# A window-attention and two-MoE kernel: rounds of 2, 7 and 7 feature blocks instead of 4, 6 and 6, and q tiles earlier in the queue

## Chip, core and metric

The kernel runs on one core of one Trainium2 chip. The metric is the device time of one execution in microseconds; a profiled execution gives a trace of every engine besides.

## What is computed

Inputs are float32. Attention has 2 batches, 8 heads, 768 positions and a head size of 64. Each position attends to the keys less than 16 positions away and to 24 block summaries (blocks of 32):

```python
k_sum = k.reshape(B, H, nb, 32, D).max(axis=3)
v_sum = v.reshape(B, H, nb, 32, D).mean(axis=3)
scores = [local q.k/8 where |i-j| < 16, q.k_sum/8 + log(32)]
a = softmax(scores)            # sum + 1e-9
x = a @ [v, v_sum]             # to 1536 tokens x 512
x = relu(x @ w_in)**2 @ w_out                    # 512 -> 2048 -> 512
xn = x / rms(x) * rms_g
out = (silu(xn @ w_gate) * (xn @ w_val)) @ w_out2  # 512 -> 1536 -> 512
```

## The kernel before

**Tokens.** The 1536 tokens are 12 groups of 128, six to a batch. Groups count from 0; group 6 is the first of batch 1. Four groups make a chunk (NCH = 3 chunks of 512 tokens).

**Attention of a group g** is a chain through four functions. scores(g) multiplies q by the group's keys, held transposed in kT (one buffer: batch 1 overwrites batch 0). softmax(g) adds the mask, takes the maximum, the exponentials and the division on VectorE and ScalarE; EXPACT chooses between eight exponentials with the sum accumulated and one long exponential. ptrans(g) transposes the probabilities on TensorE. av(g) multiplies them by vx, the group's values with the block means appended, and split_xs writes the result as a high and a low part, xhi and xlo, which is what the products consume. qload(g) and qprep(g) fetch and transpose the q of two groups; vload(g) fetches a group's rows of v into vx by six transfers; prep_load, prep_k and prep_kend make kT; vmean, its copy vm on ScalarE and vmfix (transfers from vm into vx) make the block means.

**Weights.** A unit is one feature block of 128 features of one weight matrix. It arrives as raw words of the input (512 KB) and is converted by the Units class in a pipeline: load, conv_a on ScalarE, conv_b on VectorE (four steps), split into hi and lo on both. tick() moves each unit one step; until(u) ticks until u is ready. The list `order` sets the order, round by round. load(k) issues transfers up to the k-th unit; `cap` and `used` limit how far loading runs ahead. Weights, raw words, and the q, k and v tiles share 14 buffers of one tag; nine more come free when attention's memory is released.

**Feed-forward.** All products are three matmuls (hi by hi, hi by lo, lo by hi) per 128 rows. The 16 feature blocks of the first feed-forward are split into rounds (ROUNDS1); each round goes over all tokens and adds to yp. Round 0 runs beside attention in the loop over k_ (six steps, two groups each): h_pair(k_, f) computes two blocks for two groups (256 columns each) and squares, y_pair(k_, f) multiplies by w_out. TICKS gives the conversions at the end of each k_. The later rounds (steps1) run over chunks of 512 tokens after it, and then the second feed-forward (steps2).

**Order.** Instructions are queued on each engine in the order of the program as a list scheduler arranges it at build time: where an instruction's inputs would be late, a later one can be put ahead of it. On the chip each queue runs in order. All transfers are issued by SP's queue.

Of the kernel before, what the change touches and what calls it, by code (L numbers as in the profile page):

```python
# [14 lines left out]
AF = mybir.ActivationFunctionType  # L15
# [17 lines left out]
def tile_window_attention_moe_moe2(  # L33
# [13 lines left out]
    nc = tc.nc  # L47
# [19 lines left out]
    NG = NT // P  # L67
# [3 lines left out]
    NCH = NG // MT  # L71


    ROUNDS1 = [4, 6, 6]
    ROUNDS2 = [4, 4, 4]
    FIRST1 = [sum(ROUNDS1[:r]) for r in range(len(ROUNDS1))]
    FIRST2 = [sum(ROUNDS2[:r]) for r in range(len(ROUNDS2))]
# [121 lines left out]
    class Units:  # L199


        def __init__(self, units):
# [3 lines left out]
            self.ahead = 3  # L206
            self.used, self.cap = 0, 2 * ROUNDS1[0]

# [29 lines left out]
    def PARTS(g):  # L238
        return 2 if g < 3 else 1

    QB = 2
    TICKS = (0, 0, 1, 1, 2, 3)
    WARM = 10
    WOLAG = 2
    order = [("wi", f) for f in range(ROUNDS1[0])] + [("wo", f) for f in range(ROUNDS1[0])]
    for kinds, out_, rounds, firsts in (
        (("wi",), "wo", ROUNDS1, FIRST1), (("wg", "wv"), "wp", ROUNDS2, FIRST2)
    ):
# [25 lines left out]
    mark = {}  # L274

    def after(*marks):
        es = ExitStack()
        for m in marks:
            es.enter_context(tc.issue_after(mark[m].ins))
        return es  # L280
# [73 lines left out]
    def qload(g):  # L354
        b, r = divmod(g, GPB)
        state[("q", g)] = token_chunk(q, b, r // 2, f"qr{g}")
# [11 lines left out]
    def vmean(b, c):  # L368

        if c == 0:  # L370
            state["vmps"] = psA(f"vmean{b}", [NB, DM])
        ps = state["vmps"]
        pb = BLK // 2
        nb2 = P // pb
        vr = state.pop(("v", b, c))
        for e in range(2):
            nc.tensor.matmul(
                ps, ind[:, nb2 * (NC2 - 1 - c) : nb2 * (NC2 - 1 - c) + NB], vr[:, :, e, :],
                start=(c == 0 and e == 0), stop=(c == NC2 - 1 and e == 1),
            )  # L380
        if c == NC2 - 1:
            vm = ap_.tile([NB, DM], F32, tag="vm", name=f"vm{b}", bufs=1)
            nc.scalar.copy(vm, ps)
            state["vm"] = vm
            state[("vsum", b)] = True

# [10 lines left out]
    def vload(g):  # L397
        b, r = divmod(g, GPB)
        i0 = 2 * g % NVX
        for u in range(2):  # L400
            t0 = r * P + u * QT
            for j, n, o in ((0, WIN, t0 - WIN), (K0, QT, t0), (K1, WIN, t0 + QT)):
                o = min(max(o, 0), S - n)
                nc.sync.dma_start(  # L404
                    vx[j : j + n, i0 + u], v[b, :, o : o + n, :].rearrange("h s d -> s h d")
                )
# [19 lines left out]
    def softmax(g):  # L426
        r = g % GPB
        mk = masks["first" if r == 0 else ("last" if r == GPB - 1 else "mid")]
        sl = state.pop(("s", g))
        te = ap_.tile([P, 2, NPAIR, NK], F32, tag="t", name=f"t{g}", bufs=TB)  # L430
        t = te.rearrange("q e p n -> q (e p) n")
        state[("t", g)] = t
        mx = ap_.tile([P, H], F32, tag="mx", name=f"mx{g}", bufs=TB)
        sm = ap_.tile([P, H], F32, tag="sm", name=f"sm{g}", bufs=TB)
        parts = PARTS(g)
        n = H // parts
        for i in range(parts):
            hs = slice(n * i, n * i + n)
            tv, m_, s_ = t[:, hs], mx[:, hs], sm[:, hs]
            for e in range(2 // parts * i, 2 // parts * (i + 1)):  # L440
                nc.vector.tensor_tensor(
                    te[:, e], sl[e], mk.unsqueeze(1).to_broadcast([P, NPAIR, NK]), op=ALU.add
                )
            if EXPACT(g):
                nc.vector.reduce_max(m_, tv, axis=AX.X, negate=True)
                for h in range(hs.start, hs.stop):
                    mark[("exp", g)] = nc.scalar.activation(  # L447
                        t[:, h], t[:, h], AF.Exp, bias=mx[:, h : h + 1], accum_out=sm[:, h : h + 1]
                    )
            else:  # L450
                nc.vector.reduce_max(m_, tv, axis=AX.X)
                nc.vector.tensor_tensor(tv, tv, m_.unsqueeze(2).to_broadcast([P, n, NK]), op=ALU.subtract)
                mark[("exp", g)] = nc.scalar.activation(tv, tv, AF.Exp)
                nc.vector.reduce_sum(s_, tv, axis=AX.X)
            nc.vector.tensor_scalar_add(s_, s_, 1e-9)
            nc.vector.reciprocal(s_, s_)
            mark[("norm", g)] = nc.vector.tensor_tensor(
                tv, tv, s_.unsqueeze(2).to_broadcast([P, n, NK]), op=ALU.mult
            )
# [121 lines left out]
    def group(g):  # L581

        scores(g)
        if g > 3:
            vload(g)
        softmax(g)
        if g + 2 < NG and g % 2 == 0:
            qload(g + 2)


# [12 lines left out]
    for c in range(NC2):  # L603
        vm_load(0, c)
    vload(0)
    vload(1)
    qload(2)
    for j in (0, LK - WIN):
        nc.gpsimd.memset(kT[:, :, j : j + WIN], 0.0)
    prep_k(0, 0)  # L610
# [10 lines left out]
        vmean(0, c)  # L621
    vmfix(0, NVX // 2)
    with after("vmfix"):
        units1.load(8)
    softmax(1)
    rot["tags"] = ("a", "x")
# [39 lines left out]
    def h_pair(k_, f):  # L666
        ps = psB.tile([P, CH], F32, tag="h", name=f"h0_{k_}_{f}", bufs=2)
        m = 2 * k_ % MT
        for j in range(2):
            units1.until(("wi", f + j))  # L670
            product(ps[:, G2 * j : G2 * (j + 1)], W[("wi", f + j)], xs[(1, 2 * k_ // MT)], m, m + 2)
        t = square(ps, f"0_{k_}_{f}")
        hq[(k_, f)] = hsplit(t, CH, f"0_{k_}_{f}")

    def y_pair(k_, f, between=()):
        if f == 0:
            for m in range(2):
                ys[m] = y_tile(k_, m, "y0_")
        hh = hq.pop((k_, f))
        for j in range(2):  # L680
            units1.until(("wo", f + j))
            ff_out(
                [ys[m] for m in range(2)], [t[:, G2 * j : G2 * (j + 1)] for t in hh],
                W[("wo", f + j)], f + j == 0, f + j == ROUNDS1[0] - 1,
            )
            if between:
                between[j]()
        if k_ == NK2 - 1:
            units1.used += 4
        if f == ROUNDS1[0] - 2:  # L690
            for m in range(2):
                gather(2 * k_ + m, ys.pop(m), 0, ROUNDS1, "y", None)
# [3 lines left out]
    for k_ in range(NK2):  # L696
        g, last = 2 * k_ + 3, 2 * k_ + 3 >= NG
        if k_ == 0:
            for c in range(NC2):
                prep_load(1, c)  # L700
        h_pair(k_, 0)
        if k_ == 0:
            av(2)
            group(4)
        if not last:
            ptrans(g)
        if g == GPB - 1:
            group(GPB)
        h_pair(k_, 2)
        if not last:  # L710
            av(g)
        if g == GPB - 1:
            for c in range(NC2):
                vmean(1, c)
            vmfix(0, 1)
        if g + 2 < NG:
            group(g + 2)
            if g + 2 == GPB + 1:
                vmfix(1, 1)
        y_pair(k_, 0)  # L720
        if g + 1 < NG:
            ptrans(g + 1)
        if k_ == 0:
            prep_begin(1)
            prep_k(1, 0)
            y_pair(k_, 2, (lambda: prep_k(1, 1), lambda: prep_k(1, 2)))
            prep_kend(1, 0)
            prep_kend(1, 1)
            for c in range(NC2):
                vm_load(1, c)  # L730
        else:
            if g + 3 < NG:
                qprep(g + 3)
            y_pair(k_, 2)
        if g + 1 < NG:
            av(g + 1)
        if k_ == 0:
            qprep(GPB)
        elif g + 3 < NG:
            group(g + 3)  # L740
        if k_ == 2:
            units1.cap = NW - 3
        for _ in range(TICKS[k_]):
            units1.tick()
        if not last and g == NG - 1:
            actx.close()
            rot["tags"] = ("a",)
            side["pool"] = ctx.enter_context(
                tc.tile_pool(name="w2pool", bufs=1, side="right", reuse_waits="tile")
            )  # L750
            side["psum"] = ctx.enter_context(
                tc.tile_pool(name="psY2", bufs=1, space=PSUM, reuse_waits="tile")
            )
            grow = side["pool"].tile([P, DM], F32, tag="grow", name="grow")
            nc.sync.dma_start(grow, rms_g.partition_broadcast(P))
            units1.cap = NW + NRIGHT - 3
# [4 lines left out]
    for i in range(n1 + 2):  # L761
        if i < n1:
# [3 lines left out]
            ps = psB.tile([P, CH], F32, tag="h", name=f"h{c}_{f}", bufs=2)  # L766
# [92 lines left out]
```

## Time and profile before

| | us |
|---|---|
| time, median of 3 runs | 678.31 (677.69 to 678.68) |
| the profiled execution | 682.7 |
| its span, first to last instruction | 681.0 |
| TensorE busy | 654.7 (96%) |
| VectorE busy | 404.4 (59%) |
| ScalarE busy | 305.8 (45%) |

The profiled execution is 4.4 us over the median of the timed runs, and 1.7 us of it lie outside the span. Times in the trace count from the start of the span. Busy time of TensorE is modelled, and it includes time at the lower clock, in which the same matmul takes twice as long.

### The profile page before, as it was taken

The numbers are of one execution on the slowest core, as the hardware profiler recorded it, in microseconds if no ns is written. First come the engines' busy times: TensorE is split into PE (matmuls) and PEld (weight loads), VectorE is DVE, ScalarE is ACT, GpSimd is POOL, SyncE is SP. The second block draws the span as 40 slices with busy tenths as digits, with TensorE's granted clock in tenths as the row PEclk, the third lists the DMA queues.
The fourth block names the chain that finished last, engine by engine and source line by source line (L and its number), as shares of the span: only waits on it lengthen the run. The fifth ranks groups of instructions, "written<-read, shape, count | busy, mean of one in ns | idle before, by whom it ended". The sixth has DMA issues, their size and how long they took to land.

```text
span 681.0 us, 9361 instructions
## 1 busy us (share of the span) xinstructions
PE 654.7 (96%) x3644; PEld 533.9 (78%) x3644; DVE 404.4 (59%) x733; ACT 305.8 (45%) x637; POOL 4.1 (1%) x25
## 2 busy tenths in 40 slices
PE   7768998999999999999999999999999999999997
PEld 5456957888888888888888888888888888888885
DVE  4799758656999579726574795189613171313132
ACT  4597558365866447326352773167411131111110
POOL 2000000000000000000000000000000000000000
PEclk9769998999999999999999999999999999999999
DMA  9678556222522223001021251015300000001011
GB/s 244 147 247 190 131 171 160 68 49 91 189 62 94 93 63 123 31 1 62 13 98 46 68 180 62 1 34 162 113 1 1 0 1 0 1 1 62 1 62 63
DMA packets 78188, 54.22 MB, mean 80 GB/s; under 512 B 46080, under 2 KB 72704, under 8 KB 78144
## 3 DMA queue, kind: packets, MB, share of 16 engines
q1 hardware_dynamic: 78144, 53.62, 26.7%
q8 instruction: 29, 0.48, 0.3%
q14 instruction: 15, 0.12, 0.1%
HBM read 50.07 MB, written 3.15 MB: 78 GB/s over the span
## 4 chain that ended last, share of the span: by engine, by line
PE 86%; SPq 5%; DVE 4%; DMA 2%; ACT 1%; issue 1%; DVEq 0%; ACTq 0%
PE y L530 19%; PE h L509 18%; PE g L509 15%; PE v L509 15%; PE z L530 14%; SPq L404 3%; PE xps L488 1%; PE pps L467 1%; PE s L418 1%; SPq L303 1%; DMA raw_wo<-in_moe_w_out_dram 1%; PE xps L500 1%; ACT t L447 1%; SPq L292 1%; DMA raw_wi<-in_moe_w_in_dram 1%
## 5 line engine op out<-in xcount | busy, mean ns | idle before, releaser
L509 PE MATMUL h<-xhi,w_wi 128*128 128x512 f32 (+1 forms) x480 | 136.6, 357 | 1.8 <-ACT xhi L478 1.2
L530 PE MATMUL y<-w_wo,hhi 128*128 128x512 f32 x384 | 120.7, 398 | 1.9 <-ACT hhi L520 1.7
L805 DVE TENSOR_TENSOR sg<-v,sg 128x512 f32<-128x512 f32 x36 | 24.9, 692 | 134.8 <-PE v L509 134.8
L509 PEld LDWEIGHTS h<-xhi,w_wi 128*128 128x128 f32 x480 | 87.3, 195 | 15.7 <-ACT xhi L478 1.9
L509 PE MATMUL v<-xhi,w_wv 128*128 128x512 f32 x288 | 95.6, 393 | 0.0
L509 PE MATMUL g<-xhi,w_wg 128*128 128x512 f32 x288 | 95.4, 393 | 0.0
L530 PE MATMUL z<-w_wp,hhiz 128*128 128x512 f32 x288 | 89.0, 392 | 0.0
L509 PE MATMUL h<-xlo,w_wi 128*128 128x512 f32 (+1 forms) x240 | 86.1, 359 | 1.8 <-DVE xlo L479 1.8
L530 PEld LDWEIGHTS y<-w_wo,hhi 128*128 128x128 f32 x384 | 72.4, 190 | 18.2 <-ACT hhi L520 1.9
L530 PE MATMUL y<-w_wo,hlo 128*128 128x512 f32 x192 | 75.1, 401 | 0.0
L803 ACT ACTIVATE sg<-g 128x512 f32<-128x512 f32 x36 | 21.6, 600 | 104.6 <-PE g L509 102.4
L509 PEld LDWEIGHTS v<-xhi,w_wv 128*128 128x128 f32 x288 | 54.0, 188 | 12.3
L509 PEld LDWEIGHTS g<-xhi,w_wg 128*128 128x128 f32 x288 | 54.0, 188 | 12.3
L530 PEld LDWEIGHTS z<-w_wp,hhiz 128*128 128x128 f32 x288 | 54.0, 188 | 11.9
L657 ACT ACTIVATE r<-h 128x512 f32<-128x512 f32 x48 | 28.7, 598 | 71.3 <-PE h L509 71.2
L509 PE MATMUL g<-xlo,w_wg 128*128 128x512 f32 x144 | 56.6, 393 | 0.0
L509 PE MATMUL v<-xlo,w_wv 128*128 128x512 f32 x144 | 56.5, 393 | 0.0
L530 PE MATMUL z<-w_wp,hloz 128*128 128x512 f32 x144 | 55.9, 392 | 0.0
L509 PEld LDWEIGHTS h<-xlo,w_wi 128*128 128x128 f32 x240 | 46.9, 195 | 9.0 <-DVE xlo L479 2.4
L658 DVE TENSOR_TENSOR r<-h,r 128x512 f32<-128x512 f32 x48 | 33.0, 687 | 35.0 <-ACT r L657 35.0
L520 ACT CAST hhiz<-sg 128x512 fp32r<-128x512 f32 x36 | 22.4, 621 | 69.7 <-DVE sg L805 69.4
L530 PEld LDWEIGHTS y<-w_wo,hlo 128*128 128x128 f32 x192 | 36.2, 191 | 8.1 <-issue 0.2
(125 smaller groups left out, 897.5 us busy)
## 6 DMA issues: line engine op xcount, KB each, us to landing
raw_wi<-in_moe_w_in_dram SPq DMA_DIRECT2D x16, 512.0 KB
raw_wo<-in_moe_w_out_dram SPq DMA_DIRECT2D x16, 512.0 KB
raw_wg<-in_moe_w_gate_dram SPq DMA_DIRECT2D x12, 512.0 KB
raw_wv<-in_moe_w_val_dram SPq DMA_DIRECT2D x12, 512.0 KB
raw_wp<-in_moe_w_out_dram SPq DMA_DIRECT2D x12, 512.0 KB
kr<-in_k_dram SPq DMA_DIRECT2D x12, 256.0 KB
qr<-in_q_dram SPq DMA_DIRECT2D x12, 256.0 KB
vr<-in_v_dram SPq DMA_DIRECT2D x6, 512.0 KB
```

The costliest lines, as they stand in the source:

```text
L292: nc.sync.dma_start(t.rearrange("p h e d -> p h (e d)"), src[b, :, 2 * P * c : 2 * P * (c + 1), :].rearrange("h (p e) d -> p h (e d)", e=2),)
L303: nc.sync.dma_start(t[:, j].rearrange("p (h d) -> p h d", h=H), src[b, :, o : o + P, :].rearrange("h p d -> p h d"),)
L404: nc.sync.dma_start(vx[j : j + n, i0 + u], v[b, :, o : o + n, :].rearrange("h s d -> s h d"))
L418: mark[("s", g)] = nc.tensor.matmul(sl[e][QT * u : QT * u + QT, p, :], qT[rr, p, QT * u : QT * u + QT], kT[rr, p, o : o + NK], start=True, ...
L447: mark[("exp", g)] = nc.scalar.activation(t[:, h], t[:, h], AF.Exp, bias=mx[:, h : h + 1], accum_out=sm[:, h : h + 1])
L509: nc.tensor.matmul(ps, a_, b_, start=(i == 0), stop=(i == tot - 1))
L520: nc.scalar.copy(hi[:, 0:n], s[:, 0:n])
L530: nc.tensor.matmul(y, a_[:, ms], b_, start=(first and i == 0), stop=(last and i == 2))
L657: nc.scalar.activation(t, ps, AF.Relu)
L658: nc.vector.tensor_tensor(t, ps, t, op=ALU.mult)
L803: nc.scalar.activation(t, psg, AF.Silu)
L805: nc.vector.tensor_tensor(t, psv, t, op=ALU.mult)
```

## The change

ROUNDS1 becomes [2, 7, 7]: in the loop over k_, one h_pair and one y_pair run per step instead of two each, and the two blocks join the later rounds. Since `cap` and the beginning of `order` follow ROUNDS1[0], round 0 wants four units instead of eight, and units1.load(8) then fetches wi0, wi1, wo0, wo1, wi2, wi3, wi4, wo2. The one h_pair stands behind av(2), group(4), ptrans and, at GPB - 1, group(GPB). TICKS gets one more conversion, at k_ = 1. qload(2) is issued ahead of vload(1) instead of behind it, qload(4) right behind vmfix and ahead of the raw weights instead of within group(2). Group 1's exponentials are queued on ScalarE behind the copy vm.

```diff
--- before.py
+++ after.py
@@ -71,7 +71,7 @@
     NCH = NG // MT
 
 
-    ROUNDS1 = [4, 6, 6]
+    ROUNDS1 = [2, 7, 7]
     ROUNDS2 = [4, 4, 4]
     FIRST1 = [sum(ROUNDS1[:r]) for r in range(len(ROUNDS1))]
     FIRST2 = [sum(ROUNDS2[:r]) for r in range(len(ROUNDS2))]
@@ -239,7 +239,7 @@
         return 2 if g < 3 else 1
 
     QB = 2
-    TICKS = (0, 0, 1, 1, 2, 3)
+    TICKS = (0, 1, 1, 1, 2, 3)
     WARM = 10
     WOLAG = 2
     order = [("wi", f) for f in range(ROUNDS1[0])] + [("wo", f) for f in range(ROUNDS1[0])]
@@ -380,7 +380,7 @@
             )
         if c == NC2 - 1:
             vm = ap_.tile([NB, DM], F32, tag="vm", name=f"vm{b}", bufs=1)
-            nc.scalar.copy(vm, ps)
+            mark["vm"] = nc.scalar.copy(vm, ps)
             state["vm"] = vm
             state[("vsum", b)] = True
 
@@ -450,7 +450,8 @@
             else:
                 nc.vector.reduce_max(m_, tv, axis=AX.X)
                 nc.vector.tensor_tensor(tv, tv, m_.unsqueeze(2).to_broadcast([P, n, NK]), op=ALU.subtract)
-                mark[("exp", g)] = nc.scalar.activation(tv, tv, AF.Exp)
+                with after(*(["vm"] if g == 1 else [])):
+                    mark[("exp", g)] = nc.scalar.activation(tv, tv, AF.Exp)
                 nc.vector.reduce_sum(s_, tv, axis=AX.X)
             nc.vector.tensor_scalar_add(s_, s_, 1e-9)
             nc.vector.reciprocal(s_, s_)
@@ -584,7 +585,7 @@
         if g > 3:
             vload(g)
         softmax(g)
-        if g + 2 < NG and g % 2 == 0:
+        if g + 2 < NG and g % 2 == 0 and g > 2:
             qload(g + 2)
 
 
@@ -603,8 +604,8 @@
     for c in range(NC2):
         vm_load(0, c)
     vload(0)
+    qload(2)
     vload(1)
-    qload(2)
     for j in (0, LK - WIN):
         nc.gpsimd.memset(kT[:, :, j : j + WIN], 0.0)
     prep_k(0, 0)
@@ -621,6 +622,7 @@
         vmean(0, c)
     vmfix(0, NVX // 2)
     with after("vmfix"):
+        qload(4)
         units1.load(8)
     softmax(1)
     rot["tags"] = ("a", "x")
@@ -698,15 +700,13 @@
         if k_ == 0:
             for c in range(NC2):
                 prep_load(1, c)
-        h_pair(k_, 0)
-        if k_ == 0:
             av(2)
             group(4)
         if not last:
             ptrans(g)
         if g == GPB - 1:
             group(GPB)
-        h_pair(k_, 2)
+        h_pair(k_, 0)
         if not last:
             av(g)
         if g == GPB - 1:
@@ -717,13 +717,12 @@
             group(g + 2)
             if g + 2 == GPB + 1:
                 vmfix(1, 1)
-        y_pair(k_, 0)
         if g + 1 < NG:
             ptrans(g + 1)
         if k_ == 0:
             prep_begin(1)
             prep_k(1, 0)
-            y_pair(k_, 2, (lambda: prep_k(1, 1), lambda: prep_k(1, 2)))
+            y_pair(k_, 0, (lambda: prep_k(1, 1), lambda: prep_k(1, 2)))
             prep_kend(1, 0)
             prep_kend(1, 1)
             for c in range(NC2):
@@ -731,7 +730,7 @@
         else:
             if g + 3 < NG:
                 qprep(g + 3)
-            y_pair(k_, 2)
+            y_pair(k_, 0)
         if g + 1 < NG:
             av(g + 1)
         if k_ == 0:

```

## Rows read from the trace of the kernel before

**Rows 1.** The page, part 2: TensorE's busy tenths in 40 equal slices of the span.
```profile
PE   7768998999999999999999999999999999999997
```

**Rows 2.** Table of stretches (window, its length, busy us of each engine, clock, DMA).
```profile
0.00:28.10 28.10, 19.01 (x140) 13.29 (x141) 16.91 (x38) 13.28 (x33) 4.05 (x25) 0.91 0.81 198
28.10:87.70 59.60, 51.15 (x514) 43.74 (x513) 49.27 (x90) 41.37 (x107) 0.00 (x0) 0.87 0.70 186
87.70:162.20 74.50, 70.17 (x715) 56.74 (x714) 47.27 (x79) 44.90 (x134) 0.00 (x0) 0.95 0.37 98
162.20:681.00 518.80, 514.39 (x2278) 420.17 (x2278) 290.98 (x528) 206.24 (x365) 0.00 (x0) 1.00 0.18 58
```

**Rows 3.** Chain that ended last, in order of time: start us, us, what.
```profile
22.35 3.07 DMA qr<-in_q_dram
...
40.64 1.66 SPq L404
```

**Rows 4.** Timeline of SP's queue, 0 to 70 us: start us, us, line, transfer, count.
```profile
13.75 8.56 SPq L404 DMA_DIRECT2D vx<-in_v_dram  x12
22.35 1.06 SPq L303 DMA_DIRECT2D qr<-in_q_dram  x2
...
33.36 5.27 SPq L303 DMA_DIRECT2D qr<-in_q_dram  x2
38.72 10.29 SPq L404 DMA_DIRECT2D vx<-in_v_dram  x12
```

**Rows 5.** Chain that ended last, whole span: TensorE's pieces with their counts.
```profile
85.02 2.75 PE y L530 x12
...
147.41 4.51 PE h L509 x36
...
190.20 2.80 PE h L509 x12
```

**Rows 6.** Table of stretches for tile y alone.
```profile
40.00:87.70 47.70, 13.48 (x48) 8.64 (x48) 1.26 (x2) 0.59 (x1) 0.86 0.66 159
87.70:162.20 74.50, 20.03 (x73) 13.83 (x72) 2.18 (x4) 1.75 (x3) 0.95 0.37 98
```

**Rows 7.** Groups by line up to 162.2 us, VectorE: busy, mean ns, idle before.
```profile
L658 DVE TENSOR_TENSOR r<-h,r 128x512 f32<-128x512 f32 x10 | 6.9, 686 | 4.7 <-ACT r L657 4.7
...
L186 DVE SCALAR_TENSOR_TENSOR x_wi<-raw_wi,x_wi 128x512 uint32<-128x512 uint32 x7 | 4.7, 686 | 0.0
...
L182 DVE TENSOR_SCALAR x_wi<-x_wi 128x512 f32<-128x512 f32 x7 | 2.9, 420 | 4.9 <-ACT x_wi L175 4.8
```

**Rows 8.** Timeline of all engines, 24 to 31 us.
```profile
24.31 1.17 ACT L453 ACTIVATE t<-t 128x480 f32<-128x480 f32 x2 [2.58 <-DVE t L452]
...
25.39 0.56 ACT L383 COPY vm<-vmean 24x512 f32<-24x512 f32 x1
...
30.58 0.66 DVE L441 TENSOR_TENSOR t<-s,mask_mid 128x480 f32<-128x480 f32 x1 [2.49 <-PE s L418]
```

**Rows 9.** Timeline of TensorE and VectorE, groups 6, 10 and 11.
```profile
104.56 1.27 PE L488 MATMUL xps<-pT,vx 120*64 120x64 f32 x30
...
134.28 1.21 DVE L441 TENSOR_TENSOR t<-s,mask_mid 128x480 f32<-128x480 f32 x2
...
140.65 1.16 DVE L457 TENSOR_TENSOR t<-t,sm 128x960 f32<-128x960 f32 x1
...
142.93 1.21 DVE L441 TENSOR_TENSOR t<-s,mask_last 128x480 f32<-128x480 f32 x2
```

**Rows 10.** Table of stretches around the start of the next round.
```profile
250.00:280.00 30.00, 30.00 (x131) 24.41 (x130) 28.72 (x55) 20.44 (x35) 0.00 (x0) 1.00 0.29 88
```

**Rows 11.** Table of stretches of 10 us with a low granted clock (column after POOL).
```profile
20.00:30.00 10.00, 5.09 (x30) 4.14 (x30) 7.77 (x20) 5.75 (x17) 0.00 (x0) 0.66 0.51 106
40.00:50.00 10.00, 6.74 (x31) 5.94 (x30) 9.57 (x20) 8.70 (x27) 0.00 (x0) 0.51 0.66 163
110.00:120.00 10.00, 7.76 (x76) 6.01 (x75) 7.20 (x12) 7.39 (x24) 0.00 (x0) 0.76 0.84 214
```

## Prediction

> **What bounds the kernel now.** I read the page first: the 40 slices [rows 1]. TensorE's busy tenths fall short of 9 in five of the first seven slices and in the last, nowhere else. So the span falls into a part where attention sets the pace and a part that is pure TensorE work. The table of stretches [rows 2] makes that exact. I cut it at three places: 28.1 us (VectorE ends the softmax of group 1), 87.7 us (first scores of group 6, the first of batch 1) and 162.2 us (the last time TensorE waits for anything). The reader should see that TensorE is idle 9.1 us in the first stretch (28.1 - 19.01), 8.5 us in the second, 4.3 us in the third, and then only 4.4 us in 518.8, at the very end. Call the stretches S (start), A, B and C.
>
> The chain of waits [rows 3] says why A is slow. The q tile of groups 2 and 3 lands late; later TensorE does nothing useful until the window tiles vx of groups 2 and 3 have been issued on SP's queue. SP's own order [rows 4] shows why: qr(2) goes out at 22.35, behind twelve vx transfers; the raw weights follow, and the second qr pair (5.27 us for what took 1.06 us before) and vx stand behind seven 512 KB weight transfers. VectorE is meanwhile busy 49.27 of A's 59.6 us [rows 2], much of it converting weights, since eight are wanted before the first k_ step is through.
>
> **The change, part by part.** *Feed-forward moved.* A pair of blocks for two groups is 24 matmuls of 256 columns in h_pair and 12 of 512 in y_pair. The chain has 36 of the first kind in 4.51 us, so 24 in 3.0, and 12 of the second in 2.75 [rows 5]: 5.75 us a pair. There are 12 pairs now (six k_ times two) and six after, so 6 x 5.75 = 34.5 us of TensorE leave round 0. Two blocks join the later rounds: 2 x 3 chunks x 2 products of 12 wide matmuls at 2.75 to 2.80 us, taken as 2.77, which is 33.3 us. The form alone gains 1.2 us. Where they stand now: 48 y matmuls before 87.7 (4 pairs) and 73 from there to 162.2 (6 pairs, one matmul of them into the next) [rows 6]; two pairs lie in C. Half of each goes: 11.5 from A, 17.25 from B, 5.75 from C.
>
> *Weights.* Four conversions (wi2, wi3, wo2, wo3) are no longer wanted at once. One costs VectorE 0.42 + 0.42 + 0.69 + 0.69 + 0.69 = 2.9 us [rows 7], four 11.6; a pair costs it 0.69 + 0.69 = 1.37 [rows 7], and two pairs leave A, 2.7. VectorE in A falls from 49.3 to 34.9 us. Its idle time in A is 10.3 us, of which 2.49 is the wait for group 2's scores [rows 8].
>
> *q tiles and vm.* qload(2) passes vload(1)'s six transfers, so it goes out at about 18 instead of 22.35 (half of the 8.56 us of vx x12 earlier [rows 4]). Those six vx pass 1.06 us later, and are wanted only when group 1's attention product starts, past 34 us: no cost. VectorE is busy up to 28.1 anyway, so only the 2.49 us wait goes, not the full four. The new wait puts vm's copy ahead of group 1's exponentials on ScalarE. Behind it stand those exponentials and all of ScalarE's queue; but ScalarE sits idle 2.58 us before them, and the copy takes 0.56 [rows 8], so it fits in the gap: no cost, and if vmean came later than that gap the price would be up to 0.6. It frees vmfix (four transfers, 3.5 us on SP, from 25.98 now): SP is through with vload(1) at about 23.4, so they start there, 2.5 us earlier, and end near 27. qload(4) passes the seven raw weights, which brings it from 33.36 to there. The raw weights lose about 1 us of SP time to it and gain the 2.5. The last qload leaves the place ahead of vx(2), so vx(2) should start 3 to 5 us earlier; this is inside the A estimate, not added.
>
> *h_pair(0) behind av(2) and group(4), and one more tick at k_ = 1.* Both move work within A; the tick is one conversion of 2.9 us of VectorE. Priced at nothing for TensorE, because a conversion of a later round only fills VectorE's gaps; if that cover is gone it is 2.9 us of A.
>
> *A, summed.* VectorE 34.9 + idle left 7.8 (10.3 - 2.5) = 42.8 us instead of 59.6: A ends at 70.9, 16.8 earlier. From below, TensorE: 51.15 - 11.5 = 39.7. From above: three conversions of later blocks (the x32 buffers are three) are pulled forward without their last step, 3 x 2.2 = 6.6, so 49.4. I take 42.8, by VectorE's own row. Net of the 11.5 us that only moved, A gives 5.3 us.
>
> *B, summed.* It now lasts 74.5. With the moved pairs out and the same waits it would be 57.25. From below, TensorE's floor: 57.25 - 4.3 = 52.9. From above, the softmax chains as they run now, with nothing gained: the first group has its scores at 87.7 and its attention product is over at 105.8 (104.56 + 1.27) [rows 9], because v's means come between; two 512-wide steps like those of [rows 7] follow, so 19.4 us. The other five follow at the distance of two successive groups late in B, whose masks start at 134.28 and 142.93, 8.65 apart [rows 9]; within that the softmax itself, masks to the end of the division at 141.81, takes 7.5. 19.4 + 5 x 8.65 = 62.6. I take 59.0, nearer the upper end, because the means' transfers and product come earlier with A but get no shorter. That loses 1.75 us against 57.25.
>
> *C.* 518.8 - 5.75 + 33.3 = 546.3. A round now needs 14 weights instead of 12, two more conversions, 5.8 us, where VectorE was busy 28.72 of 30 us around a round's start [rows 10]: at worst 5.8 - 1.3 = 4.5 us. TensorE is busy all 30 us there and in C as a whole to its end [rows 2], so the weights come ahead of need, and I take zero.
>
> **Sum.** 28.1 + 42.8 + 59.0 + 546.3 = 676.2 us of span against 681.0: -4.8. The profiled run took 682.7, 4.4 above the median of the runs, so 677.9 on its scale and 678.3 - 4.8 = 673.5 on the median's.
>
> **The rivals.** (1) *Batch 1's attention loses its cover and sets the pace in B; slower.* For: now TensorE is idle only 4.3 us there, so the feed-forward does hide the softmax chain, and half of that goes. Against: VectorE is busy 47.27 and ScalarE 44.9 of 74.5 us [rows 2], so engines have room. Decides when B exceeds 57.25 + 5.3 + 1.2 = 63.75 us: with 19.4 for the first group, a period of 8.9. At a period of 10, B is 69.4 and the time 673.5 + 10.4 = 683.9.
>
> (2) *The clock falls with the cover; slower.* In three stretches of 10 us the granted clock was 0.66, 0.51 and 0.76 [rows 11], and the first of them holds the wait for qr [rows 3]. The loss is half of the busy time spent at 1.2 GHz: shares 0.68, 0.98 and 0.48 of 5.09, 6.74 and 7.76 us, or 1.7 + 3.3 + 1.9 = 6.9 us. If as much again is lost where attention now runs thinner, the time is 673.5 + 6.9 = 680.4. For: two of the three lie where little feed-forward is ready yet. Against: B as a whole is granted 0.95 [rows 2]. The Trainium skill (TensorE: Matmul & The Clock Gate, Loop structure matters more than you think) has the same rule: matmuls in dense succession keep the full clock, a wait between bursts loses it; by that rule a thinner attention stage ends slower, and the trace's 40 to 50 us agree with it, at 0.51.
>
> (3) *The front doesn't move; no change.* The transfers of vx(2) stay behind the raw weights, which still number seven, and VectorE fills itself with conversions (A 49.4, 6.6 more, or no gain from the queue at all). A then gives about nothing and the time is 673.5 + 5.3 = 678.8. For: SP issues in order. Against: group 4's scores need only its q tile, which moves ahead.
>
> (4) *B runs at TensorE's floor.* B 52.9, the time 673.5 - 6.1 = 667.4. For: engines' room as in (1), and round 1's first h products can fill gaps once their weights exist.
>
> **Chances.** The forecast (A shorter, B about as well covered) 0.42, its own range 670 to 676.5; rival 4 0.18; rival 3 0.15; rival 1 0.17; rival 2 0.08. A difference under 0.2% (1.4 us) can hardly be told from none here. So faster 0.60, same 0.15, slower 0.25. The range is 666 to 681.5: it takes in rivals 2, 3 and 4 and the lower part of 1, and leaves out a B paced at 10 us and a C that stalls.
>
> **What would show it.** Right: qr(2) issued near 18 us and vm's copy ahead of group 1's exponentials; VectorE's 2.49 us wait gone; first scores of group 6 near 71 us; the last TensorE wait near 130, and a C of about 546 without idle time; 144 matmuls of 256 columns on h. Wrong: group 6 past 76, or B over 63.75 with TensorE waiting for pT or xhi, or granted clocks near 0.5 between 71 and 130, or waits of TensorE for weights after the last group.

## The result, and the profile after

The change made the kernel slower: 690.0 us, median of 4 runs (689.45 to 691.21), against 678.5 for the kernel before; the ratio is 1.0137 with a 95% interval of 1.0103 to 1.0171. The profiled execution after is its median, with a span of 688.3 us; that of before, at 682.7, lay 4.2 us above the median of 678.5, so the two traces differ by 7.3 us where the medians differ by 11.5.

TensorE's busy time is the same in both traces, 655.1 us against 654.7. What grew is its idle time, from 26.3 (681.0 - 654.7) to 33.2 us. The 40 slices of the page after [rows 1]:

```profile
PE   7776969989999999999999999999999999999997
```

The table of stretches after (window, its length, busy us of PE, PEld, DVE, ACT, POOL, then clock, DMA share, GB/s), cut where its own stages end: first scores of group 6 at 75.4, end of TensorE's last wait and the matmul behind it at 147.6:

```profile
0.00:28.10 28.10, 20.88 (x168) 14.03 (x170) 17.57 (x39) 14.15 (x35) 4.03 (x25) 0.97 0.84 204
28.10:75.40 47.30, 36.09 (x404) 30.83 (x400) 41.53 (x79) 34.96 (x96) 0.00 (x0) 0.84 0.91 235
75.40:147.60 72.20, 62.15 (x656) 49.08 (x656) 56.65 (x97) 50.18 (x145) 0.00 (x0) 0.95 0.42 113
147.60:688.30 540.70, 536.01 (x2351) 436.56 (x2349) 289.60 (x520) 208.69 (x365) 0.00 (x0) 1.00 0.16 54
```

Read length minus PE in each row and set it beside [rows 2]: idle 7.2 (was 9.1) in S, 11.2 (8.5) in A, 10.1 (4.3) from there to the last wait, 4.7 (4.4) behind it. Of the 10.1 us, 8.0 lie before group 11's xlo is done at 137.7, which is where B ends as the prediction cuts it, and 2.0 are one wait behind it. A is 12.3 us shorter, but more work than that left it: 48 of its 96 h matmuls and 36 of its 48 y matmuls, 14.25 us at the prediction's prices. The idle time grew in A and nearly doubled in B.

The edits to the start did what they say. SP's queue after [rows 4]:

```profile
18.07 1.33 SPq L303 DMA_DIRECT2D qr<-in_q_dram  x2
...
23.38 3.46 SPq L393 DMA_DIRECT2D vx<-vm  x4
26.89 1.13 SPq L303 DMA_DIRECT2D qr<-in_q_dram  x2
...
34.66 4.92 SPq L404 DMA_DIRECT2D vx<-in_v_dram  x6
```

qr(2) goes out at 18.07, vmfix at 23.38, qr(4) at 26.89, and vx of group 2 at 34.66 instead of 38.72. On ScalarE and VectorE [rows 8], the timeline of 17 to 31 us:

```profile
20.98 0.58 ACT L383 COPY vm<-vmean 24x512 f32<-24x512 f32 x1
...
23.55 1.17 ACT L454 ACTIVATE t<-t 128x480 f32<-128x480 f32 x2 [1.99 <-DVE t L452]
...
27.24 0.65 DVE L441 TENSOR_TENSOR t<-s,mask_mid 128x480 f32<-128x480 f32 x1
...
29.38 0.66 DVE L441 TENSOR_TENSOR t<-s,mask_mid 128x480 f32<-128x480 f32 x1 [1.49 <-PE s L418]
```

The copy vm stands ahead of group 1's exponentials, and group 2's mask starts at 27.24 instead of 30.58; VectorE's 2.49 us wait is 1.49 us, for the second half of the scores.

Where the new idle time is, TensorE's timeline shows (in brackets the idle time ahead of the instruction and what ended it):

```profile
44.17 1.04 PE L418 MATMUL s<-kT,qT 64*64 64x120 f32 x16 [2.79 <-ACT qT L365]
...
52.85 0.65 PE L468 MATMUL pps<-ident,t 128*120 128x128 f32 x4 [1.39 <-DVE xlo L480]
...
59.92 1.97 PE L489 MATMUL xps<-pT,vx 120*64 120x64 f32 x30 [5.43 <-ACT pT L469]
...
98.52 0.62 PE L468 MATMUL pps<-ident,t 128*120 128x128 f32 x4 [1.52 <-DVE t L458]
103.11 0.47 PE L489 MATMUL xps<-pT,vx 120*64 120x64 f32 x2 [3.97 <-ACT pT L469]
126.29 1.21 PE L531 MATMUL y<-w_wo,hhi 128*128 128x512 f32 x4 [1.58 <-ACT hhi L521]
...
147.00 0.50 PE L510 MATMUL h<-xhi,w_wi 128*128 128x512 f32 x1 [2.03 <-DVE r L660]
```

All but the last wait for a link of attention's chain or of a feed-forward pair that hangs on it. The two longest come from the order of ScalarE's queue. Its timeline ahead of 59.92:

```profile
51.82 0.68 ACT L176 ACTIVATE u_wi<-raw_wi 128x512 int32<-128x512 uint32 x1
54.60 0.67 ACT L175 ACTIVATE x_wi<-raw_wi 128x512 f32<-128x512 f32 x1 [2.10 <-DVE w_wo L196]
...
56.26 0.40 ACT L447 ACTIVATE t<-t,mx 128x120 f32<-128x120 f32 x1
...
59.30 0.56 ACT L469 COPY pT<-pps 120x512 f32<-120x512 f32 x1
```

TensorE ended group 3's transposes at 53.50 (52.85 + 0.65), but their copy pT starts at 59.30, behind steps of weight conversions, one of which waits 2.10 us, and behind group 4's eight exponentials. Ahead of 103.11:

```profile
98.15 0.57 ACT L479 CAST xhi<-xps 128x512 fp32r<-128x512 f32 x1
101.92 0.66 ACT L176 ACTIVATE u_wo<-raw_wo 128x512 int32<-128x512 uint32 x1 [3.20 <-DMA raw_wo<-in_moe_w_out_dram]
102.49 0.57 ACT L469 COPY pT<-pps 120x512 f32<-120x512 f32 x1
```

A weight conversion of a later round stands ahead of group 7's pT copy, and the queue waits 3.20 us for its raw words. No run changes the order of ScalarE's queue alone, so what these two waits, 9.4 us of TensorE's idle time, are worth stays open.

### The profile page after: what moved, and what is told of

Same layout as the page of the kernel before. It is cut to its first block, busy times and chain, and to the rows that moved or that the text cites. A ratio compares the mean times of both kernels' runs of the same rounds, so it can differ in the third digit from the quotient of the medians.

```text
span 688.3 us, 9226 instructions
## 1 busy us (share of the span) xinstructions
PE 655.1 (95%) x3572; PEld 530.5 (77%) x3572; DVE 405.4 (59%) x733; ACT 308.0 (45%) x639; POOL 4.0 (1%) x25
## 4 chain that ended last, share of the span: by engine, by line
PE 82%; DVE 6%; ACT 5%; DMA 2%; SPq 2%; issue 1%; DVEq 0%; ACTq 0%
PE y L531 19%; PE h L510 17%; PE v L510 14%; PE z L531 14%; PE g L510 13%; PE s L418 1%; PE xps L489 1%; PE pps L468 1%; ACT t L447 1%; SPq L303 1%; DVE t L441 1%; SPq L393 1%; DMA raw_wo<-in_moe_w_out_dram 1%; PE xps L501 1%; DMA raw_wi<-in_moe_w_in_dram 1%
## 5 line engine op out<-in xcount | busy, mean ns | idle before, releaser
L510 PE MATMUL h<-xhi,w_wi 128*128 128x512 f32 (+1 forms) x432 | 130.4, 369 | 2.7 <-DVE r L660 2.0
L510 PEld LDWEIGHTS h<-xhi,w_wi 128*128 128x128 f32 x432 | 78.6, 189 | 17.8 <-DVE r L660 2.2
L510 PE MATMUL h<-xlo,w_wi 128*128 128x512 f32 (+1 forms) x216 | 80.1, 371 | 0.0
L659 ACT ACTIVATE r<-h 128x512 f32<-128x512 f32 x48 | 28.5, 597 | 78.2 <-PE h L510 78.2
L510 PEld LDWEIGHTS v<-xhi,w_wv 128*128 128x128 f32 x288 | 54.0, 188 | 12.3
L531 PEld LDWEIGHTS z<-w_wp,hhiz 128*128 128x128 f32 x288 | 54.1, 188 | 11.9
L510 PEld LDWEIGHTS h<-xlo,w_wi 128*128 128x128 f32 x216 | 40.7, 188 | 7.0
```

The source lines that it names most:

```text
L510: nc.tensor.matmul(ps, a_, b_, start=(i == 0), stop=(i == tot - 1))
L531: nc.tensor.matmul(y, a_[:, ms], b_, start=(first and i == 0), stop=(last and i == 2))
L659: nc.scalar.activation(t, ps, AF.Relu)
```

## The experiments

In the expectations, theory A says that with half the feed-forward gone attention's own chains set the pace of the front; theory B, that the weight conversions pulled forward hold the softmaxes up on VectorE; theory C, that the rounds alone cost the time and the edits to the start give a little; theory S, that the edits to the start are what costs. Later letters are explained with their runs. "Front" is the time at which group 11's attention product ends on TensorE: 160.8 us before, 136.4 after. These are its last products on TensorE's timeline and its xlo on VectorE's, before and then after:

```profile
159.67 1.15 PE L488 MATMUL xps<-pT,vx 120*64 120x64 f32 x30
161.47 0.69 DVE L479 TENSOR_TENSOR xlo<-xps,xhi 128x512 fp32r<-128x512 f32 x1 [1.46 <-ACT xhi L478]
...
134.30 2.08 PE L489 MATMUL xps<-pT,vx 120*64 120x64 f32 x62
137.03 0.69 DVE L480 TENSOR_TENSOR xlo<-xps,xhi 128x512 fp32r<-128x512 f32 x1 [0.20 <-ACT xhi L479]
```

"Lost time" is worked out from stretches of 1 us up to 180 us, TensorE's idle time plus half-clock loss (busy time by one minus the granted clock): 21.9 + 10.8 us before, 28.5 + 9.4 after. Every ratio is to runs of the kernel before on the same chip, whose times lay between 677.05 and 685.35.

**The two halves of the change.** The start alone is the kernel before with

```diff
-    vload(1)
     qload(2)
+    vload(1)
...
     with after("vmfix"):
+        qload(4)
         units1.load(8)
```

and vm ahead of group 1's exponentials; the rounds alone are the changed kernel without these.

> The kernel before (rounds of 4, 6, 6) with only the edits of the start: q tiles earlier, vm's copy ahead of group 1's exponentials. Theory C (the rounds alone cost the time, the start's edits give a little): 675 to 677 us, ratio 0.996 to 0.999, since the trace of the changed kernel shows VectorE's 2.5 us wait for group 2's scores gone. Theory S (the start's edits are what costs): over 683 us, ratio 1.007 or more.

> The changed kernel without the edits of the start: rounds of 2, 7, 7, order of h_pair and ticks only. Theory C: 691 to 694 us, ratio 1.018 to 1.023, the start's edits being worth 1 to 3 us. Theory S: 680 us or less, ratio 1.003 or less.

Measured: start alone 685.37 us, 1.0079 (1.0038 to 1.0120), front 162.2; rounds alone 691.66 us, 1.0182 (1.0137 to 1.0228), front 137.9. So the larger loss comes with the rounds, as theory C has it, and theory S falls, which had the rounds alone at 680 or less. But theory C's other half falls too: the start's edits cost 0.8% where they stand alone, and within the whole change their effect isn't told apart (the intervals of 1.0137 and 1.0182 overlap). Alone, they cut TensorE's idle time to 15.9 us, 6.0 less, but the half-clock loss rose by 5.5 to 16.3. The table of stretches of that run:

```profile
46.00:48.00 2.00, 2.00 (x18) 1.63 (x14) 1.09 (x3) 2.00 (x5) 0.00 (x0) 0.50 0.56 127
48.00:50.00 2.00, 2.00 (x21) 1.30 (x19) 1.97 (x5) 2.00 (x4) 0.00 (x0) 0.50 0.87 195
50.00:52.00 2.00, 2.00 (x7) 1.47 (x8) 2.00 (x6) 0.73 (x2) 0.00 (x0) 0.50 1.18 265
52.00:54.00 2.00, 2.00 (x12) 2.00 (x11) 2.00 (x5) 1.23 (x2) 0.00 (x0) 0.50 0.95 214
```

TensorE is busy in all 8 us and is granted 0.50, 1.2 GHz. By 180 us the start alone has done 12 wide matmuls fewer than the kernel before (6 of h and 6 of y, 2.8 us), though TensorE idled less. The single executions agree: at a mean granted clock of 0.975 and 0.978 the start alone took 685.57 and 683.37 us, the kernel before on that chip 685.35, and 682.12 and 683.40. The loss of the rounds is there at the same clock: at 0.980 the rounds alone took 689.68 and 691.03 us, the kernel before 682.78 to 684.26.

**Which of the start's edits.** The kernel before with qload(2) and vm moved, qload(4) left where it was:

> The kernel before (4, 6, 6) with qload(2) ahead of vload(1) and vm's copy ahead of group 1's exponentials, but qload(4) left where it was. The start's edits together cost 0.8%: TensorE's idle time fell by 6 us up to 180 us, but its busy time at 1.2 GHz grew, with a granted clock of 0.50 from 46 to 54 us. If the early q tile of group 2 brings that, 682 to 687 us; if it is the move of qload(4), 675 to 680 us, and this version may beat both kernels.

681.54 us, 1.0018 (0.9995 to 1.0040), front 159.0, lost time 17.6 + 10.6: no measurable change, and a time between the two ranges expected. So the cost of the start points to the early qload(4), though the intervals of 1.0018 and 1.0079 just overlap. How it brings the longer spell at 1.2 GHz wasn't traced further.

**Conversions.** Both kernels with the four VectorE steps of each weight conversion left out (what follows computes with wrong weights):

```diff
+        return x
         nc.vector.tensor_scalar(x, x, HW_MIN, HW_MAX, op0=ALU.max, op1=ALU.min)
```

> The kernel before with the four VectorE steps of conv_b left out of every weight conversion (2.2 of 2.9 us of VectorE each; the weights are then wrong numbers). It is the base for the next run. Both theories: TensorE waited 21.8 us up to 162.2 us, part of it for converted weights between 40 and 70 us, so 668 to 674 us, ratio 0.985 to 0.994.

> The changed kernel with the same four VectorE steps left out of every conversion. Theory A (half the feed-forward gone leaves the softmax chains of batch 1 uncovered, whatever else VectorE does): still 8 to 14 us slower than the run before_noconv. Theory B (the four conversions that moved from the front in among the softmaxes hold these up in the in-order queues): no slower than before_noconv by more than 3 us, perhaps faster by 5.

676.44 us, 0.9929 (0.9900 to 0.9959), 2.4 above the range expected, and 688.3 us, 1.0130 (1.0083 to 1.0178). The two kernels remain 11.9 us apart, and theory B falls for these four steps; ScalarE's steps of the conversions were left in. The kernel before gains: its A ends at 79.1 instead of 87.7. The changed kernel's A ends at 74.0 instead of 75.4:

```profile
28.10:74.00 45.90, 40.01 (x412) 34.62 (x411) 30.46 (x54) 36.28 (x99) 0.00 (x0) 0.78 0.93 238
```

VectorE is now busy only 30.46 of the 45.9 us, and TensorE's idle time there fell from 11.2 to 5.9 us. But the granted clock fell from 0.84 to 0.78, so that TensorE was busy 40.01 us instead of 36.09 with 412 matmuls instead of 404. So VectorE's steps held A before the change; after it, taking them out shortens A by 1.4 us, with the clock in the way.

**Attention without feed-forward beside it.** The changed kernel with no h_pair and no y_pair in the loop over k_ (zeros in yp; conversions kept), so round 0's two blocks are missing from the result:

> The changed kernel with round 0's feed-forward left out altogether (no h_pair, no y_pair; zeros are added in their place); the conversions stay. Six pairs of 5.6 us, 34 us of TensorE, go. In the changed kernel the attention product of group 11 ends at 136.4 us. Theory A (the softmax chains pace the attention part, the feed-forward only fills gaps): it ends at 122 to 132 us, so that less than half of the 34 us comes back. Theory T (TensorE still paces it, and its queue is what attention stands in): it ends at 102 to 112 us.

672.99 us (one run), span 671.3. The front ends at 141.2, not earlier than the 136.4 with two blocks and later than either theory had it. About 27.4 us of round 0's 34.5 lay ahead of that end in the changed kernel (7.1 behind it); here 14.1 us of round 1's h products (48 matmuls) were drawn into the gaps between 60 and 100 us, so that some 13 us of work are gone without a gain, and behind 100 us there is no feed-forward at all until the front has ended. Its stretches from 28.1 us, with the last 41 us by themselves in the fourth row and batch 1's part in the fifth:

```profile
28.10:60.00 31.90, 23.01 (x272) 18.86 (x272) 25.65 (x51) 23.40 (x73) 0.00 (x0) 0.71 0.92 237
60.00:80.00 20.00, 15.62 (x102) 12.56 (x102) 19.18 (x34) 13.49 (x28) 0.00 (x0) 0.80 0.90 243
80.00:141.20 61.20, 47.16 (x524) 35.85 (x524) 38.29 (x65) 37.20 (x120) 1.00 (x2) 0.80 0.46 129
...
100.00:141.20 41.20, 28.74 (x354) 24.00 (x352) 22.05 (x34) 21.91 (x80) 1.00 (x2) 0.71 0.32 80
85.90:141.20 55.30, 41.59 (x497) 31.60 (x496) 32.39 (x51) 31.97 (x110) 1.00 (x2) 0.78 0.44 123
```

The front is late partly for what happens in batch 0: group 6's scores start at 85.9 us instead of 75.4, with VectorE busy 19.18 of the 20 us from 60 to 80. Batch 1's part by itself, from there to the front, took 73.1 us with four blocks (87.7 to 160.8), 61.0 with two (75.4 to 136.4) and 55.3 with none. The last step took 72 h and 37 y matmuls out of it, about 17.5 us, for 5.7, and the granted clock there fell from 0.94 to 0.78. This decides against theory T and for theory A in batch 1, though not by the time it gave.

Behind 100 us no engine is busy more than 70% (28.74 of 41.2), and some of that is at 1.2 GHz. The reader sees a chain of latencies and no full engine. The summary of waits, 75 to 142 us (who waited <- for whom: us in total, times, longest), agrees; each link waits for the one before it:

```profile
ACT xhi L479 <- PE xps L489: 11.3, 6, 4.9
...
DVE t L441 <- PE s L418: 9.1, 4, 4.2
PE pps L468 <- DVE t L458: 8.9, 3, 4.3
DVE sm L456 <- ACT t L447: 8.0, 4, 2.6
```

The three kernels make a series. With four blocks beside attention the span is 681.0, with two 688.3, and with none it would be 671.3 + 33.3 (two more blocks at the later rounds' price) = 704.6, an estimate from one run: there the second pair of blocks taken out costs more than the first.

**Buffers and transfers that might hold attention.** Three score buffers instead of two (TB = 3), in both kernels; banks of PSUM, the memory that TensorE writes its products to, shared by a third tag; and no v transfers for groups 4 to 11 (these groups compute with stale v):

```diff
-    NW, NRIGHT, RAWS, TB = 14, 9, 5, 2
+    NW, NRIGHT, RAWS, TB = 14, 9, 5, 3
...
-    rot["tags"] = ("a", "x")
+    rot["tags"] = ("a", "x", "h")
...
-        if g > 3:
-            vload(g)
```

> The changed kernel with three buffers instead of two for the probabilities and their sums (TB). In the changed kernel's trace the masks of group 9 wait 2.15 us for the transposes of group 7. Theory A with this buffer as the gate: 683 to 687 us. Theory A with the chain's own work as the pace: 688 to 692 us, no change from 690.

> The kernel before with three buffers for the probabilities. Its feed-forward covers the chain, so every theory expects no change: 677 to 683 us, ratio 0.997 to 1.003. It is the base for after_tb3.

> The changed kernel with the two PSUM banks of tag h shared with attention's scores, transposes and products (h is used half as often now). Four TensorE waits in the changed kernel's trace are for a bank that VectorE or ScalarE still reads (1.25, 2.79, 1.39, 1.47 us; 6.9 in sum). Banks as the gate: 682 to 687 us. Otherwise 688 to 693 us.

> The changed kernel without the transfers that load v into vx for groups 4 to 11 (48 of them; those groups then use old values). Theory L: group 11's product ends at 131 to 137 us, next to no change. Theory V: at 115 to 127 us.

Measured: changed kernel with three buffers 689.72 us, 1.0131 (1.0090 to 1.0172), front 136.9; kernel before with three 681.68 us, 1.0001 (0.9972 to 1.0030), front 160.4; shared banks 698.23 us, 1.0261 (1.0215 to 1.0307), front 142.4, worse; no v transfers 689.36 us (one run), front 136.0. The third buffer and the v transfers alone don't move the front, though with either edit TensorE's idle time up to 180 us fell (22.7 and 22.5 instead of 28.5) and the half-clock loss rose (16.4 and 13.2 instead of 9.4). The shared banks made it worse than either range expected; why wasn't traced, so whether banks hold attention stays open.

**A shorter chain.** Maximum and subtraction left out, one long exponential for every group, in both kernels (the results are then wrong):

```diff
-                nc.vector.reduce_max(m_, tv, axis=AX.X)
-                nc.vector.tensor_tensor(tv, tv, m_.unsqueeze(2).to_broadcast([P, n, NK]), op=ALU.subtract)
-                mark[("exp", g)] = nc.scalar.activation(tv, tv, AF.Exp)
+                mark[("exp", g)] = nc.scalar.activation(tv, tv, AF.Exp, scale=0.125)
```

> The changed kernel with a shorter softmax: the maximum and its subtraction are left out, and one long exponential takes the place of the eight short ones in every group (the row sums are made by VectorE). A group's chain loses about 2 us of latency (1.15 for the maximum, 2 of 3 on the exponentials, 1.15 back for the sum) and ScalarE 3.7 us a group in nine of twelve. Theory L (the softmax chains, by their latency or ScalarE's share, pace the attention part): group 11's product ends at 118 to 127 us instead of 136.4 and the time is 676 to 683 us. Theory V (the transfers of v into vx pace it): it ends past 132 us, 686 us or more.

> The kernel before with the same shorter softmax. TensorE paces its attention part from 88 us on, so theory L expects little: 673 to 680 us, so that the two roundings come within 4 us of each other. Theory V: 676 to 682 us, the changed one 8 us or more behind it.

685.99 us, 1.0070 (1.0045 to 1.0095), front 131.6, and 676.72 us, 0.9939 (0.9912 to 0.9965), front 151.6. A shorter chain helps both, but the changed kernel's front fell by 4.8 us only, less than expected, and the front of the kernel before by 9.2. So the length of the chain is a part of the answer, and the kernel before also waits for it. Theory L as written fails: it had the two kernels within 4 us of each other, and they are 9.3 apart, which is what theory V had. The run without v transfers, with its front at 136.0, speaks against theory V in turn.

**How many groups are under way.** In the run without feed-forward, group 10 needs 14.8 us from its scores (122.7) to its product (137.5), the least of batch 1's six (groups 7 and 8 need 23.7), and groups 6 to 11 end 7.2 us apart (105.1 to 141.2, five steps): two at a time, which is how the loop queues them, group(g + 2) behind av(g). The next edit queues scores and softmax one group ahead from the third k_ step on (with TB = 3):

```diff
+        if k_ >= 2 and g + 2 < NG:
+            scores(g + 2)
+            softmax(g + 2)
         if not last:
             ptrans(g)
...
+        if k_ >= 2 and g + 2 < NG:
+            vload(g + 2)
+        if k_ >= 2 and g + 3 < NG:
+            qprep(g + 3)
+            scores(g + 3)
+            softmax(g + 3)
+            if g + 5 < NG:
+                qload(g + 5)
```

> The changed kernel with three buffers for the scores (TB = 3) and, from the third k_ step on, the scores and softmax of the next group queued ahead of the transposes of the present one, so that three groups instead of two are under way in the queues (groups 9, 10 and 11; their v transfers stay behind the product that frees their place). Theory D (depth): what is left as attention's own length is the length of one group's chain, near 15 us from scores to product in the run without feed-forward, divided by the two groups that the order of the queues lets overlap. Then group 11's product ends 5 to 10 us earlier than the 136.4 us of the changed kernel, at 126 to 131, and the time falls by 4 to 9 us, to 681 to 686. Theory E (each group's work on the engines, whatever the order): group 11's product ends at 134 to 139 and the time stays within 2.5 us of 690.

> The kernel before with the same reordering. Theory D: with four blocks TensorE sets the pace in batch 1 (idle 4.3 us between 87.7 and 162.2), so the order gives at most what is idle after 130 us: the end of group 11's product stays at 157 to 161 us and the time within 2 us of the kernel before. Theory E: the same. It is run to see whether the order beats the kernel before at all.

> The kernel without round 0's feed-forward products (zeros in their place) with the same reordering. Its attention ended at 141.2 us with no engine full after 100 us. Theory D: 128 to 135. Theory E: 139 to 144.

> As the run before, and besides it the four VectorE steps of each weight conversion and the v transfers of groups 4 to 11 left out. If depth is what counts (theory D), this gives little more than the order alone, under 5 us. If several resources each hold attention at about the same length (theory F: taking any one away leaves the next), only this run falls clearly, by over 10 us below 141.2.

Measured: changed kernel 687.93 us, 1.0086 (1.0058 to 1.0114), front 131.6; kernel before 678.51 us, 0.9961 (0.9931 to 0.9991), front 150.2; without feed-forward 668.22 us (one run), front 134.5; the same without conversions and v transfers 664.04 us (one run), front 132.3. The last products on TensorE's timeline, first of the run without feed-forward in the old order, then in the new one:

```profile
137.39 1.96 PE L468 MATMUL pps<-ident,t 128*120 128x128 f32 x8
139.29 0.48 PE L489 MATMUL xps<-pT,vx 120*64 120x64 f32 x2
140.03 1.15 PE L489 MATMUL xps<-pT,vx 120*64 120x64 f32 x30 [0.27 <-ACT pT L469]
```

```profile
128.08 0.48 PE L489 MATMUL xps<-pT,vx 120*64 120x64 f32 x2 [1.28 <-ACT pT L469]
129.87 1.97 PE L489 MATMUL xps<-pT,vx 120*64 120x64 f32 x30
...
133.38 1.15 PE L489 MATMUL xps<-pT,vx 120*64 120x64 f32 x32 [0.68 <-ACT pT L469]
```

Theory D holds for the front without feed-forward, where the edit takes 6.7 us off (the third buffer wasn't run by itself there). In the changed kernel it takes 4.8 off, just short of the range expected, and TensorE's idle time in B falls from 8.0 to 3.7 us:

```profile
74.60:133.00 58.40, 54.66 (x611) 41.70 (x611) 46.15 (x78) 43.80 (x133) 0.00 (x0) 0.97 0.45 122
```

Little of that is seen in the time: 687.93 is 1.9 us above theory D's range and inside theory E's, and the intervals of 1.0086 and 1.0137 overlap. With the conversions' VectorE steps and the v transfers gone as well, only another 2.2 us go, so theory F (several resources, each enough) falls by the condition set for it. But idle time fell there from 33.2 to 28.0 us and the half-clock loss rose from 16.0 to 20.0, so what these resources would hold at the full clock isn't shown.

My expectation for the kernel before was wrong: I had it paced by TensorE, and its front came 10.6 us earlier. Its lost time fell from 32.7 to 26.3 (20.25 + 6.01), and the two traces differ by 6.2 us; but the trace of before is of an execution above its median and this one of an execution below it, and the medians differ by 2.9 us, 0.4%. It is the one version here with the same computation that beats both kernels, and it keeps four blocks.

## Why the prediction was wrong

**The step that failed** is that waits were held fixed while work was taken out. For B the prediction says it outright, "with the moved pairs out and the same waits it would be 57.25", and the 59.0 of its sum stays near that; for A it is "VectorE 34.9 + idle left 7.8". It takes work and waits as terms that can be subtracted one by one. Instead waits grew in the work's place: TensorE's idle time rose from 8.5 to 11.2 us in A and from 4.3 to 8.0 in B. The 28.75 us of TensorE work that were to leave A and B (11.5 and 17.25) brought group 11's xlo from 162.2 to 137.7, only 24.5 us earlier, and what lies behind it grew from 518.8 to 550.6, since the later rounds pay the two blocks in full: -24.5 and +31.8 are the 7.3 us of the traces. The sum had -32.3 and +27.5.

This is rival 1 by its mechanism, attention losing its cover, but not by its condition, B over 63.75, nor by its price, 683.9: A and C missed by more than B, 4.5 and 4.3 us against 3.3. The runs show how B's waits hang on the order of attention's queue (8.0 us of idle time became 3.7 with one more group queued ahead). How A's 4.5 us divide among the chains, ScalarE's queue and the clock stays open.

On the medians' scale the miss is 16.5 us (690.0 against 673.5). Of these, 4.4 are the distance of the kernel before's profiled execution from the median of its first three runs, which the forecast carried over; after the change the profiled execution is the median. The other 12.1 us (688.3 against 676.2), span by span:

*S*, 28.1, as cut. The queue edits are as predicted in each place (18.07, 23.38, the copy ahead of the exponentials). VectorE's wait for group 2's scores fell to 1.49 us instead of going. The gain of these edits isn't to be found in the time.

*A* lasted 47.3, not 42.8: +4.5, the largest of the three. The upper bound of 49.4 was nearer. VectorE's busy time was 41.53, the 34.9 of the sum plus 6.6, the size of the term of the three conversions pulled forward that I kept for the range: where the sum took out four conversions, the third of the steps (L186) still ran six times in A, and seven times before. But these steps are not all of it: with VectorE at 30.46 us A still took 45.9, at a lower clock. Taking the engine that bounds A before as the one that bounds it after was the error. Net of the work that only moved, 14.25 us and not the 11.5 of the sum, A gave nothing, where 5.3 was forecast. A reading ahead of the sum was wrong as well: while the window tiles vx of groups 2 and 3 were issued, from 38.72 to 49.01 [rows 4], TensorE was not without useful work, but busy 6.74 of the 10 us from 40 to 50 [rows 11].

*B*, to group 11's xlo at 137.7, lasted 62.3, not 59.0: +3.3, close to the 62.6 that I had worked out from the chains as they ran. That it comes so close is partly luck: the first group took 25.3 us to its xlo and not 19.4, the other five 7.4 each and not 8.65. The threshold of 63.75 wasn't passed; it counted on A's 5.3.

*C* lasted 550.6, not 546.3: +4.3. At 137.7 there are 24 h matmuls of 256 columns (3.0 us) and 18 of y (4.1) of round 0 left, 1.4 more than the 5.75 taken. The wait ahead of 147.00 is 2.03: two more conversions for round 1 were taken at zero with a bound of 4.5, while VectorE had no room there (busy all 9.90 us from 137.7 to 147.6). Its timeline ahead of that wait:

```profile
145.06 0.68 DVE L196 TENSOR_TENSOR w_wi<-x_wi,w_wi 128x512 fp32r<-128x512 f32 x1
145.67 0.68 DVE L189 CUSTOM_DVE_ANT_0 x_wi<-x_wi,u_wi 128x1024 uint16<-128x1024 uint16 x1
146.27 1.28 DVE L660 TENSOR_TENSOR r<-h,r 128x512 f32<-128x512 f32 x2
```

The square r, which the next h product needs done, queues behind weight steps. VectorE's room is not all of it, however: in the changed kernel without the four VectorE steps the same wait is longer:

```profile
145.81 0.50 PE L511 MATMUL h<-xhi,w_wi 128*128 128x512 f32 x1 [3.32 <-DVE r L661]
```

In both runs the Relu on ScalarE that comes ahead of the square stands behind weight steps as well. That the two more conversions cause the wait isn't shown. Another 0.3 lies at the end of the span; about 0.6 I can't place.

**The other rivals.** Rival 2, the clock: half-clock loss up to 180 us was 9.4 after and 10.8 before, so it isn't the cause of this result, and the 75 to 148 us stretch is granted 0.95 as before. Most of the start's loss, where that stands alone, goes with it. The Trainium skill (TensorE: Matmul & The Clock Gate, Loop structure matters more than you think) says that matmuls stay warm when they follow each other closely and go cold in a wait. The rows of the start alone agree with the second part, since the stretch at 1.2 GHz begins behind a wait of 2.56 us; but in the 8 us that are shown, matmuls that followed each other closely ran at 0.50 throughout. Rival 3, a front that doesn't move, was near the truth for A, with its 6.6 us of conversions and no net gain, though its other reason, SP's queue, doesn't hold: the transfers did move. Rival 4, B at TensorE's floor of 52.9, is refuted by B's 62.3 us with 8.0 of them idle.

**What stays open.** With three groups in flight and no feed-forward, groups 6 to 11 end 6.0 us apart (104.4 to 134.5), not at a third of 14.8, 4.9; what holds the rest wasn't found. Batch 0's part, which ends with group 5's product at 83.5 us after the change, was not reordered, and what holds it wasn't tried either. Nor was an order of ScalarE's queue in which the pT copies pass the weight steps. And several edits that take away one resource lowered TensorE's idle time and raised its half-clock loss, so they may understate what that resource would hold at the full clock.

## What to carry to other kernels

An engine that is 94% busy in a stretch may be busy with filler. Before taking the filler out, ask how long the chain beside it takes with nothing in its way, its least latency for one item divided by the items in flight: near that length the stage shrinks by less than the work that leaves it (here 12.1 us for the first two blocks and 5.7 for the other two, with about 17 us of work each), while the moved work is paid in full elsewhere. Waits don't stay as they are when work is removed, so an end of the range worked out from the chains as they run deserves as much weight as one worked out from busy times. If such a stage is to get shorter, another item in flight is one thing to try first; here that gave 0.4% with the cover left in place.

## What the runs showed of the hardware that was not expected

TensorE ran at 1.2 GHz while it was busy in every microsecond: granted 0.50 from 46 to 54 us in the run with the start alone, which ran transposes, attention products, scores and then h matmuls of 256 columns there, at 0.41 us each instead of the 0.28 of the same line at full clock. The wait ahead of that stretch, and the same line at either clock:

```profile
45.44 1.87 PE L418 MATMUL s<-kT,qT 64*64 64x120 f32 x16 [2.56 <-ACT qT L365]
...
53.11 0.41 PE L510 MATMUL h<-xlo,w_wi 128*128 128x256 f32 x1
...
55.53 0.28 PE L510 MATMUL h<-xlo,w_wi 128*128 128x256 f32 x1
```

Less idle time therefore didn't mean less time lost: idle fell by 6.0 us and the half-clock loss rose by 5.5. The same program also varies with it: the kernel before took 677.62 us in an execution with a mean granted clock of 0.987 and 685.35 in one with 0.975, on the same chip.
